# First MLP by Strassen's seven products in two tiles instead of five, with work that waits one step behind

## The chip, the cores and the metric

The kernel runs on one core of a Trainium2 chip. The metric is the device time of one execution in microseconds (us); lower is better. Before the change it is 1857.77 us, the median of three runs (1857.09 to 1859.08).

## What is computed

Linear attention over 8 batches of 8 heads (sequence 576, head size 64), whose output, 4608 tokens by 512, goes through two MLPs, all in float32:

```python
q_s = softmax over the head size of q;  k_s = softmax over the sequence of k
kv = einsum('bhsd,bhse->bhde', k_s, v);  x = einsum('bhsd,bhde->bhse', q_s, kv)   # 4608 x 512
xn = x / sqrt(mean(x * x) + 1e-6) * rms_g
g, val = xn @ w_gate, xn @ w_val                                                   # 512 x 1536 each
x = (silu(g) * val) @ w_out                                                        # 1536 x 512
h = x @ w_in; out = (h * sigmoid(1.702 * h)) @ w2_out                              # 512 x 2048, 2048 x 512
```

## The kernel before, in words

TensorE (PE) multiplies in a short float format, so each float32 factor is split into a high and a low half and each product takes three passes (high x high, high x low, low x high). VectorE (DVE), ScalarE (ACT) and GpSimd (POOL) make the halves, the sums and the nonlinear functions; SyncE (SP) issues most DMAs.

The tokens go in nine tiles of 512, numbered 0 to 8 here as in the code. A tile of the first MLP takes one of two forms.

A **plain tile** has 36 slots, three for each of the 12 blocks of 128 hidden columns: `hidden` for the gate (12 matmuls of 512 columns, L587), `hidden` for the value, then four output parts (`out1_parts`, 12 matmuls of 512 columns, also L587).

A **Strassen tile** (`strassen_tile`, L857) takes the first layer as 7 products of half blocks instead of 8. Its 6 groups `m` have 7 steps `k` each, in the order of products `p` = 1, 6, 5, 2, 7, 4, 3; a step is 12 matmuls of 256 columns (L893). After them the step's code goes to the other engines: DVE adds the product into the running sums `h` (L906), ACT takes silu of one half (L870), DVE multiplies it with the other (L871), ACT and DVE split the result `u` (L875, L879). `PARTS` says how many output parts PE does in each step. Tiles 3 to 7 are of this form (`FIRST`, `LAST`); three PSUM banks serve the products, one (`ps_att`) the attention. In plain tiles the products have two and the attention two.

Beside tile j the attention of four units (two heads of one batch each, `unit_steps`) makes the rows that the tile after needs, as nine steps s0 to s8: m of k (L364), a transpose (L371) and maxima (L375, L378), a second transpose (L383) and k less its maximum (L384), the exponentials (L402) and the quotient (L408 to L411), the product of k and v (s4, L417) and its halves (L425 to L434), transposes of q (L447) and their halves (L460, L461), and the attention product (L470 to L472), whose copy `xr` (L478) is ACT's. The tables `AT` and `AT7` place these steps in slots or steps; `EARLIER` and `ahead` move them up. `norm_steps` then squares, sums (L542), inverts (L548) and scales (L560) the tile's rows, and `split_x` (L579) or `x_sum`, `x_high` and `x_low` make the factors of the next tile.

Strassen tiles need sums of weights, made once in plain tiles by 12 `prepare_steps` (POOL L753, L760; ACT L666; DVE L667, one per prep) and stored to DRAM; before the change six of them lie in tile 1 and six in tile 2. Everything is issued in the order in which the Python code runs; each engine takes its own instructions in that order. Tile 8 and the second MLP (from L982 on) follow.

Of the kernel before, what the change touches and what calls it, by code (L numbers as in the profile page):

```python
# [20 lines left out]
def attention_glu_mlp(  # L21
# [26 lines left out]
    nc = tc.nc  # L48
# [32 lines left out]
    FIRST, LAST = 3, NTILE - 2  # L81
# [211 lines left out]

    units = [(b, c) for b in range(B) for c in range(NC)]
# [57 lines left out]
    def unit_steps(u, tag="att"):  # L352
# [16 lines left out]
        def s1():  # L369
# [5 lines left out]
            nc.vector.reduce_max(out=m, in_=t[:, 0:P], axis=AX.X)  # L375
            st["m"] = m
            qm = ap.tile([P, 2, R, 1], F32, tag="qm", bufs=2, name="qm")
            nc.vector.tensor_reduce(out=qm, in_=qt[u], op=ALU.max, axis=AX.X)  # L378
            side.tensor_tensor(qt[u], qt[u], qm.to_broadcast([P, 2, R, D]), op=ALU.subtract)

        def s2():
            t = bank(tag)
            nc.tensor.transpose(t[:, 0:P], st["m"].to_broadcast([P, P]), ident)  # L383
            nc.vector.tensor_tensor(  # L384
                kt[u],
                kt[u],
                t[:, 0:P]
                .rearrange("p (h o d) -> p h o d", h=2, o=1)
                .to_broadcast([P, 2, R, D]),
                op=ALU.subtract,  # L390
            )

        def s3():
# [12 lines left out]
            qe = st["q"]  # L406
            qs = ap.tile([P, R, 2, 1], F32, tag="qs", bufs=2, name="qs")
            nc.vector.tensor_reduce(out=qs, in_=qe, op=ALU.add, axis=AX.X)  # L408
            nc.vector.tensor_scalar_add(qs, qs, EPS_SUM)
            nc.vector.reciprocal(out=qs, in_=qs)  # L410
            side.tensor_tensor(qe, qe, qs.to_broadcast([P, R, 2, D]), op=ALU.mult)  # L411

        def s4():
            t = bank(tag)
            for r in range(R):
                for h in range(2):
# [26 lines left out]
        def qT(i):  # L443
# [17 lines left out]
            nc.vector.tensor_tensor(lo, t[:, :width], f(hi), op=ALU.subtract)  # L461
# [27 lines left out]
    def norm_steps(j):  # L489
        st = {}  # L490

        def squares(c):
# [3 lines left out]
            else:  # L496
# [32 lines left out]
        def halves_of_squares():  # L529
# [4 lines left out]
            nc.vector.tensor_tensor(st["h"][1], st["a"], f(st["h"][0]), op=ALU.subtract)  # L534

        def total():
# [7 lines left out]
            invert(0)  # L544
# [26 lines left out]
    def x_room(o):  # L571
        w = sp.tile([P, 2 * T + 16], F32R, tag="xs", bufs=4, name="xs")
# [1009 lines left out]
```

## Time and profile before

| | |
|---|---|
| median of three runs | 1857.77 us |
| the profiled execution | 1859.59 us, span 1857.8 us |
| busy: PE, PE weight loads, DVE, ACT, POOL | 93%, 84%, 68%, 47%, 31% of the span |
| the chain that ended last | PE 70%, DVE 15%, ACT 7%, DMA 3%, issue 3%, POOL 2% |
| tile 0; tiles 1 to 8; second MLP | 162.15; 980.13; 715.5 us |

The tiles' borders are the first matmul of each tile's first layer. A busy PE is not PE at its peak, since the ends of matmuls are modelled: the table of stretches gives PE 112.75 of 122.42 us in tile 2, in which PE's own work, back to back, is shorter. In the rows of stretches the engines stand in the order PE, PEld (weight loads), DVE, ACT, POOL; PEclk is the granted clock as a share of the full one. A wait is the idle time of an engine before an instruction, with what ended it.

### The profile page before, as it was taken

To read this page: it belongs to the slowest core of one execution; us is meant where nothing else is said; L and a number is where in the kernel's file an instruction comes from. 1 tells how busy PE (TensorE), PEld (TensorE's weight loads), DVE (VectorE), ACT (ScalarE), POOL (GpSimd) and SP (SyncE) were. 2 spreads that over 40 slices of the span, in tenths; PEclk is the share of its full clock that TensorE was granted. 3 is DMA by queue.
4 is the path that set the end of the run, shared out by engine and by line. 5 is a ranking of instruction groups with operands and counts; after the bars stand their busy time and mean duration, and the time that the engine had idled before them with its cause. 6 is when DMAs were issued, how large, how long until landed. Compare 5 with 4: busy or idle time off the path is not lost.

```text
span 1857.8 us, 29833 instructions
## 1 busy us (share of the span) xinstructions
PE 1733.6 (93%) x11082; PEld 1563.1 (84%) x11082; DVE 1266.1 (68%) x2079; ACT 865.3 (47%) x1491; POOL 570.1 (31%) x510
## 2 busy tenths in 40 slices
PE   6999898987988898888999999999999999999998
PEld 4666786777877787777888888999999999999998
DVE  7997878875575676675645435655555788887776
ACT  6775445445445554454333234544444643333332
POOL 5875735762252252242321162311000510000000
PEclk9999999999999999999999999999999999999999
DMA  6664534546455555554453303455434574444442
GB/s 164 189 184 127 173 110 147 174 133 184 146 171 172 163 164 174 155 174 128 119 153 114 125 30 119 162 177 180 149 128 137 190 241 130 145 135 131 131 126 80
DMA packets 292129, 275.65 MB, mean 148 GB/s; under 512 B 63504, under 2 KB 273424, under 8 KB 291984
## 3 DMA queue, kind: packets, MB, share of 16 engines
q1 hardware_dynamic: 281856, 255.92, 44.7%
q10 hardware_dynamic: 10128, 17.83, 2.6%
q8 instruction: 87, 1.43, 0.3%
q14 instruction: 58, 0.48, 0.1%
HBM read 189.27 MB, written 84.41 MB: 147 GB/s over the span
## 4 chain that ended last, share of the span: by engine, by line
PE 70%; DVE 15%; ACT 7%; DMA 3%; issue 3%; POOL 2%; SPq 0%; ACTq 0%; DVEq 0%; POOLq 0%
PE ps_out L1494 19%; PE ps_in L997 19%; PE ps_gv L587 9%; PE ps_acc L587 8%; PE ps_gv L893 7%; PE ps_third L893 5%; DVE h L906 2%; ACT L402 1%; DMA w2d<-w 1%; DVE m L364 1%; DVE s L871 1%; DVE qs L408 1%; PE ps_acc L615 1%; DVE xr L560 1%; DVE sqa L548 1%
## 5 line engine op out<-in xcount | busy, mean ns | idle before, releaser
L997 PE MATMUL ps_in<-xf,w2i 128*128 128x384 f32 x2016 | 350.3, 335 | 0.0
L997 PEld LDWEIGHTS ps_in<-xf,w2i 128*128 128x128 f32 x2016 | 349.9, 188 | 0.3 <-ACT h L1009 0.2
L587 PE MATMUL ps_acc<-u,wo 128*128 128x512 f32 x1152 | 311.7, 402 | 4.6 <-DVE u L879 4.0
L1494 PE MATMUL ps_out<-w2o,uf 128*128 128x256 f32 x2268 | 271.4, 281 | 0.0
L1494 PEld LDWEIGHTS ps_out<-w2o,uf 128*128 128x128 f32 x2268 | 269.5, 188 | 1.1
L186 POOL TENSOR_TENSOR wo<-raw,wo 128x512 fp32r<-128x512 f32 x96 | 133.1, 1387 | 408.2 <-ACT wo L185 337.7
L587 PEld LDWEIGHTS ps_acc<-u,wo 128*128 128x128 f32 x1152 | 207.7, 193 | 42.6 <-DVE u L879 6.5
L587 PE MATMUL ps_gv<-xs,wg 128*128 128x512 f32 x576 | 147.4, 403 | 5.5 <-DVE xs L579 4.8
L587 PE MATMUL ps_gv<-xs,wv 128*128 128x512 f32 x576 | 143.4, 396 | 1.4 <-POOL wv L186 1.4
L587 PEld LDWEIGHTS ps_gv<-xs,wg 128*128 128x128 f32 x576 | 108.2, 190 | 34.6 <-DVE xs L579 5.9
L587 PEld LDWEIGHTS ps_gv<-xs,wv 128*128 128x128 f32 x576 | 106.0, 188 | 26.0 <-POOL wv L186 2.9
L982 ACT ACTIVATE h<-h 128x384 f32<-128x384 f32 x144 | 74.2, 525 | 110.9 <-DVE h L1021 88.9
L870 ACT ACTIVATE s<-h 128x256 f32<-128x256 f32 x90 | 37.5, 417 | 170.5 <-DVE h L906 170.5
L182 POOL TENSOR_TENSOR w<-w,stage 128x512 int32<-128x512 int32 x56 | 76.0, 1357 | 121.0 <-DMA wv<-w1s_v 34.3
L663 DVE TENSOR_TENSOR raw<-raw 128x256 f32<-128x256 f32 (+1 forms) x236 | 106.2, 492 | 9.3 <-DMA raw<-w2d 7.3
L906 DVE TENSOR_TENSOR h<-h,ps_gv 128x512 f32<-128x512 f32 x100 | 68.1, 681 | 62.2 <-PE ps_gv L893 61.3
L1021 DVE TENSOR_TENSOR h<-h,ps_in 128x384 f32<-128x384 f32 x144 | 77.8, 553 | 48.0 <-PE ps_in L997 47.8
L1082 ACT ACTIVATE uf<-raw 128x1792 fp32r<-128x1792 f32 (+2 forms) x38 | 61.6, 1623 | 83.4 <-DVE raw L663 42.8
L1494 PE MATMUL ps_out<-w2oq,uf 128*128 128x256 f32 x756 | 90.9, 281 | 0.0
L1494 PEld LDWEIGHTS ps_out<-w2oq,uf 128*128 128x128 f32 x756 | 90.1, 188 | 0.0
L1086 DVE TENSOR_TENSOR uf<-raw,uf 128x1792 fp32r<-128x1792 f32 (+2 forms) x38 | 73.0, 1924 | 17.9 <-ACT uf L1082 17.9
L1317 ACT ACTIVATE s<-ps_gv 128x512 f32<-128x512 f32 x48 | 28.7, 599 | 115.8 <-PE ps_gv L587 115.7
(246 smaller groups left out, 3194.4 us busy)
## 6 DMA issues: line engine op xcount, KB each, us to landing
u<-h SPq DMA_DIRECT2D x192, 192.0 KB, 1.9
wg<-w1s_g SPq DMA_DIRECT2D x120, 256.0 KB, 3.9
wv<-w1s_v SPq DMA_DIRECT2D x120, 256.0 KB, 4.1
stage<-in_moe_w_out_dram SPq DMA_DIRECT2D x28, 512.0 KB, 3.7
raw<-u SPq DMA_DIRECT2D x24, 512.0 KB, 4.4
x<-ev ACTq DMA_DIRECT2D x34, 256.0 KB, 3.2
stage<-in_moe_w_in_dram SPq DMA_DIRECT2D x16, 512.0 KB, 3.8
w2d<-w SPq DMA_DIRECT2D x32, 256.0 KB, 5.0
```

Source lines behind the costliest of these rows:

```text
L182: return scaled, signed, lambda: nc.gpsimd.tensor_tensor(dst, dst, lo, op=ALU.add)
L186: nc.gpsimd.tensor_tensor(dst[:, 1, :], src, f(dst[:, 0, :]), op=ALU.subtract)
L587: nc.tensor.matmul(t, w(a), x(e), start=first and i == 0, stop=last and i == 2)
L663: engine.tensor_tensor(raw[:, o], raw[:, a], raw[:, b], op=op)
L893: nc.tensor.matmul(t[:, i * Q : (i + 1) * Q], w[:, a, c * P : (c + 1) * P], xs[j, p][0][c][:, e, :], start=p in (1, 6, 5, 4) and i == 0 an ...
L906: add = lambda o, a, t=both: nc.vector.tensor_tensor(o, a, t, op=ALU.add)
L982: nc.scalar.activation(dst, src, AF.Gelu_apprx_sigmoid)
L997: nc.tensor.matmul(t, w[:, a, s, c * P : (c + 1) * P], xfac[i, p, c][:, e, :], start=p in (1, 6, 5) and c == 0 and k == 0, stop=c == 1 and ...
L1021: nc.vector.tensor_tensor(v, v, t, op=ALU.add)
L1082: nc.scalar.activation(ufac[k][:, 0, piece], uraw[k][:, 1:8][:, piece], AF.Copy)
L1086: nc.vector.tensor_tensor(w[:, 1, piece], raw[:, piece], f(w[:, 0, piece]), op=ALU.subtract)
L1494: nc.tensor.matmul(t[:, i * Q : (i + 1) * Q], u[:, a, LEFT[p] - 1, i * P : (i + 1) * P], w[:, e, m % 2, :], start=m == 0 and i == 0 and n ...
```

## The change

Tiles 3, 4 and 5 become plain tiles; 6 and 7 stay Strassen tiles. The 12 preps lie three each in tiles 1 to 4, in slots 0 to 3, 8 to 11 and 16 to 19. In Strassen tiles `soon` puts DVE's and POOL's share of an attention step (and what follows the squares) into the next step's code, there behind that step's own add; the quotient goes two steps behind. Silu, product, high half and low half of `h` go to one later step each (`after_next`), except for product 2, whose silu and multiplication stay in its own step. `EARLIER` is 10 instead of 6 in Strassen tiles, so s4 follows product 2 (k=3) instead of product 1 (k=0); the tile before the first Strassen tile keeps 6, and plain tiles in front of plain ones have 0. The four inversions and the scaling of a Strassen tile are spread over more steps, `PARTS` starts one step later, and the rooms of the split x lose 64 bytes of padding.

```diff
-    FIRST, LAST = 3, NTILE - 2
+    FIRST, LAST = 6, NTILE - 2
...
+    late = {"now": [], "steps": False}
+
+    def soon(fn):
+
+        if late["steps"]:
+            late["now"].append(fn)
+        else:
+            fn()
+
+    def run_late():
+        now, late["now"] = late["now"], []
+        for fn in now:
+            fn()
...
-            nc.vector.reduce_max(out=m, in_=t[:, 0:P], axis=AX.X)
             st["m"] = m
-            qm = ap.tile([P, 2, R, 1], F32, tag="qm", bufs=2, name="qm")
-            nc.vector.tensor_reduce(out=qm, in_=qt[u], op=ALU.max, axis=AX.X)
-            side.tensor_tensor(qt[u], qt[u], qm.to_broadcast([P, 2, R, D]), op=ALU.subtract)
+
+            def maxima():
+                nc.vector.reduce_max(out=m, in_=t[:, 0:P], axis=AX.X)
+                qm = ap.tile([P, 2, R, 1], F32, tag="qm", bufs=2, name="qm")
+                nc.vector.tensor_reduce(out=qm, in_=qt[u], op=ALU.max, axis=AX.X)
+                side.tensor_tensor(
+                    qt[u], qt[u], qm.to_broadcast([P, 2, R, D]), op=ALU.subtract
+                )
+
+            soon(maxima)
...
-            nc.vector.tensor_tensor(
-                kt[u],
...
-                op=ALU.subtract,
+            soon(
...
+                    op=ALU.subtract,
+                )
             )
...
-            qe = st["q"]
...
-            side.tensor_tensor(qe, qe, qs.to_broadcast([P, R, 2, D]), op=ALU.mult)
+
+            def divide():
+                qe = st["q"]
+                qs = ap.tile([P, R, 2, 1], F32, tag="qs", bufs=2, name="qs")
+                nc.vector.tensor_reduce(out=qs, in_=qe, op=ALU.add, axis=AX.X)
+                nc.vector.tensor_scalar_add(qs, qs, EPS_SUM)
+                nc.vector.reciprocal(out=qs, in_=qs)
+                side.tensor_tensor(qe, qe, qs.to_broadcast([P, R, 2, D]), op=ALU.mult)
+
+            soon(lambda: soon(divide))
...
+            soon(lambda: kv_halves(t))
+
+        def kv_halves(t):
...
-            nc.vector.tensor_tensor(lo, t[:, :width], f(hi), op=ALU.subtract)
+            soon(lambda: nc.vector.tensor_tensor(lo, t[:, :width], f(hi), op=ALU.subtract))
...
-                side.tensor_tensor(st["a"], st["a"], sq, op=ALU.add)
+                soon(lambda: side.tensor_tensor(st["a"], st["a"], sq, op=ALU.add))
             if j >= 2 and c == NC - 1:
-                halves_of_squares()
+                soon(halves_of_squares)
...
-            invert(0)
+            if not late["steps"]:
+                invert(0)
...
-        w = sp.tile([P, 2 * T + 16], F32R, tag="xs", bufs=4, name="xs")
+        w = sp.tile([P, 2 * T], F32R, tag="xs", bufs=4, name="xs")
...
-            w = x_room(8).rearrange("p e (c t) -> p e c t", c=2)
+            w = x_room(0).rearrange("p e (c t) -> p e c t", c=2)
...
-    PARTS = (0, 1, 1, 2, 1, 1, 2)
...
+    PARTS = (0, 0, 1, 2, 1, 2, 2)
...
-            nc.scalar.activation(half, h[:, 0], AF.Silu)
-            return lambda: nc.vector.tensor_tensor(half, half, h[:, 1], op=ALU.mult)
+            return (
+                lambda: nc.scalar.activation(half, h[:, 0], AF.Silu),
+                lambda: nc.vector.tensor_tensor(half, half, h[:, 1], op=ALU.mult),
+            )
+
+        def after_next(*fns):
+
+
+            def one():
+                fns[0]()
+                if fns[1:]:
+                    after_next(*fns[1:])
+
+            late["now"].append(one)
...
-                later = []
+                end = []
+                now, late["now"] = late["now"], []
...
-                    later.append(hidden_part(s[1], 0, h["c1"]))
+                    after_next(*hidden_part(s[1], 0, h["c1"]))
...
-                    later.append(hidden_part(s[0], 1, both))
+                    silu, mult = hidden_part(s[0], 1, both)
+                    silu()
+                    end.append(mult)
...
-                    later.append(hidden_part(s[i], o, h[name]))
                     n, half = 2 * m + i, s[i]
-                    later.append(lambda n=n, half=half: split_high(n, half))
-                    later.append(
-                        lambda n=n, half=half: late["now"].append(lambda: split_low(n, half))
-                    )
-                run_late()
-                late["now"] += later
+                    silu, mult = hidden_part(half, o, h[name])
+
+                    def finish(mult=mult, n=n, half=half):
+                        mult()
+                        split_high(n, half)
+
+                    after_next(silu, finish, lambda n=n, half=half: split_low(n, half))
+                for fn in now:
+                    fn()
                 for _ in range(PARTS[k]):
                     if parts:
...
-                    if 7 * m + k == (4, 5, 7, 8)[c]:
+                    if 7 * m + k == (5, 6, 7, 8)[c]:
...
                 for fn in plan(7 * m + k):
+                    fn()
+                for fn in end:
                     fn()
                 aside(k)
...
-        EARLIER = 6
+        EARLIER = 10
...
-                put7(j, 35 - EARLIER, total)
-                for i in (1, 2, 3):
-                    put7(j, 35 + (i + 1) // 2 - EARLIER, invert, i)
-                put7(j, 36 - EARLIER, spread, False)
+                put7(j, 36 - EARLIER, total)
+                for i in range(4):
+                    put7(j, 37 + i - EARLIER, invert, i)
+                put7(j, 40 - EARLIER, spread, False)
                 for c in range(NC):
-                    put7(j, 37 + c // 2 - EARLIER, scale, c)
+                    put7(j, 41 + c // 2 - EARLIER, scale, c)
                 continue
-            ahead = EARLIER if by_strassen(j + 1) else 0
+            ahead = 6 if by_strassen(j + 1) else 0
...
-                put(FIRST - 1, 30 + i, x_sum, FIRST, p)
+                put(FIRST - 1, 29 + i, x_sum, FIRST, p)
...
-                x_low(FIRST, p, nc.gpsimd)
+                x_low(FIRST, p, nc.vector if p == 3 else nc.gpsimd)
...
+            put(FIRST - 1, 35, x_early, 3)
...
-                decode_aside()
+                decode_aside_soon()
...
+            late["steps"] = by_strassen(j)
...
-                        x_high(j + 1, 3)
-                        x_low(j + 1, 3, nc.gpsimd)
```

On DVE at the end of tile 1, where tile 2's input is inverted (L548, after the change L582), scaled (L560, now L594) and split (L579, now L613), there stands before:

```order
L378 TENSOR_REDUCE qm<-q_sb 128x10
L379 TENSOR_TENSOR q_sb<-q_sb,qm 128x640
L548 RECIPROCAL sqa<-sqa 128x128 x3
L384 TENSOR_TENSOR k_sb<-k_sb,ps_att 128x640
L176 TENSOR_SCALAR w_2660<-w_2660 128x512
L177 SCALAR_TENSOR_TENSOR w_2660<-stage,w_2660 128x512
L560 SCALAR_TENSOR_TENSOR xr<-xr,g_sb,sqa 128x512 x4
L408 TENSOR_REDUCE qs<-qe 128x10
L409 TENSOR_SCALAR qs<-qs 128x10
L410 RECIPROCAL qs<-qs 128x10
L411 TENSOR_TENSOR qe<-qe,qs 128x640
L579 TENSOR_TENSOR xs<-xr,xs 128x512 x4
```

and now:

```order
L582 RECIPROCAL sqa<-sqa 128x128
L1391 TENSOR_TENSOR s<-s,ps_gv 128x512
L637 CAST u<-s 128x512
L638 TENSOR_TENSOR u<-s,u 128x512
L582 RECIPROCAL sqa<-sqa 128x128 x3
L176 TENSOR_SCALAR w_2606<-w_2606 128x512
L177 SCALAR_TENSOR_TENSOR w_2606<-stage,w_2606 128x512
L594 SCALAR_TENSOR_TENSOR xr<-xr,g_sb,sqa 128x512 x4
L613 TENSOR_TENSOR xs<-xr,xs 128x512 x4
```

The next unit's maximum, its k and its quotient no longer stand between the inversion and the split; tiles 2 and 3 end in the same way now, while the end of tile 4 reads as that of tile 1 did.

On DVE in tile 6, around the halves of the product of k and v (`rs`, `kvH`, `kvL`), there stands before:

```order
L503 TENSOR_TENSOR sqa<-sqa,sqb 128x512
L879 TENSOR_TENSOR u<-s,u 128x512
L871 TENSOR_TENSOR s<-s,h 128x256
L425 TENSOR_SCALAR rs<-ps_att 128x1
L426 RECIPROCAL rs<-rs 128x1
L429 TENSOR_SCALAR kvH_78<-ps_att,rs 64x64 x2
L434 SCALAR_TENSOR_TENSOR kvL_80<-ps_att,rs,kvH_78 64x64 x2
L906 TENSOR_TENSOR h<-h,ps_gv 128x512
L879 TENSOR_TENSOR u<-s,u 128x512
L461 TENSOR_TENSOR qL<-ps_att,qH 128x320
```

and now:

```order
L899 TENSOR_TENSOR s<-s,ps_third 128x256
L946 TENSOR_TENSOR h_7332<-h,ps_gv 128x512
L946 TENSOR_TENSOR h<-h_7332,ps_gv 128x512
L454 TENSOR_SCALAR rs<-ps_att 128x1
L455 RECIPROCAL rs<-rs 128x1
L458 TENSOR_SCALAR kvH_79<-ps_att,rs 64x64 x2
L463 SCALAR_TENSOR_TENSOR kvL_81<-ps_att,rs,kvH_79 64x64 x2
L946 TENSOR_TENSOR h_7332<-h_7332,ps_third 128x512
L490 TENSOR_TENSOR qL<-ps_att,qH 128x320
```

The halves stood ahead of the add of product 6 (`h<-h,ps_gv`); they now stand behind both adds of product 7.

On ACT in tile 6, around the exponentials of k and q (L402, now L424), there stands before:

```order
L478 ACTIVATE xr<-ps_att 128x64
L478 ACTIVATE xr<-ps_att 128x256
L402 ACT_TABLE_LOAD
L402 ACTIVATE ke<-k_sb 128x2x5x64
L402 ACTIVATE qe<-q_sb 128x2x5x64
L870 ACT_TABLE_LOAD
L870 ACTIVATE s<-h 128x256
L875 ACTIVATE u<-s 128x512
L478 ACTIVATE xr<-ps_att 128x256
L501 ACTIVATE sqb<-xr 128x512
```

and now:

```order
L507 ACTIVATE xr<-ps_att 128x64
L507 ACTIVATE xr<-ps_att 128x256
L424 ACT_TABLE_LOAD
L424 ACTIVATE ke<-k_sb 128x2x5x64
L424 ACTIVATE qe<-q_sb 128x2x5x64
L507 ACTIVATE xr<-ps_att 128x256
L530 ACTIVATE sqb<-xr 128x512
L898 ACT_TABLE_LOAD
L898 ACTIVATE s<-ps_third 128x256
```

The copy `xr` of the second half of the attention rows stood behind a table load, a silu (`s<-h`) and a high half (`u<-s`); it now follows the exponentials.

On PE in tile 6, around the product of k and v (L417, now L443) and the transposes of q (L447, now L476), there stands before:

```order
L893 MATMUL ps_gv<-xs,wg_553 128x256 x6
L893 MATMUL ps_gv<-xs,wv_601 128x256 x6
L417 MATMUL ps_att<-v_sb_82,ke 64x65 x10
L893 MATMUL ps_gv<-xs,wg_663 128x256 x6
L893 MATMUL ps_gv<-xs,wv_695 128x256 x6
L587 MATMUL ps_acc<-u,wo 128x512 x3
L447 MATMUL ps_att<-ident,qe 128x128 x3
```

and now:

```order
L932 MATMUL ps_third<-xs,wg_942 128x256 x6
L932 MATMUL ps_third<-xs,wv_994 128x256 x6
L621 MATMUL ps_acc<-u,wo 128x512 x6
L443 MATMUL ps_att<-v_sb_83,ke 64x65 x10
L932 MATMUL ps_gv<-wg_1242,wg_842 128x256 x3
L932 MATMUL ps_gv<-wv_1281,wg_842 128x256 x3
L932 MATMUL ps_gv<-wg_1242,wv_881 128x256 x3
L932 MATMUL ps_gv<-wv_1281,wv_881 128x256 x3
L621 MATMUL ps_acc<-u,wo 128x512 x3
L476 MATMUL ps_att<-ident,qe 128x128 x3
```

The product of k and v stood behind product 1 and now stands behind product 2 and two output parts; the transposes stood behind product 6 and one part, now behind product 7 and one part.

## Rows read from the trace of the kernel before

**Rows 1.** Stretches, tiles 1 to 8: us, busy (count) by engine, PEclk, DMA, GB/s

```profile
162.15:282.62 120.47, 115.12 (x585) 90.15 (x584) 90.92 (x134) 60.02 (x95) 63.98 (x54) 0.99 0.44 138
282.62:405.04 122.42, 112.75 (x547) 89.64 (x546) 102.40 (x142) 59.04 (x94) 75.38 (x60) 0.99 0.48 154
405.04:539.19 134.15, 111.25 (x772) 100.00 (x770) 85.75 (x152) 65.23 (x117) 53.11 (x43) 0.94 0.55 164
539.19:672.39 133.20, 114.57 (x784) 102.44 (x782) 87.43 (x156) 67.33 (x125) 46.81 (x36) 0.94 0.56 165
672.39:805.17 132.78, 114.55 (x784) 102.48 (x782) 87.56 (x156) 67.09 (x125) 46.82 (x36) 0.94 0.55 167
805.17:934.00 128.83, 112.61 (x781) 100.68 (x780) 78.93 (x147) 61.67 (x118) 40.67 (x31) 0.95 0.47 137
934.00:1037.13 103.13, 97.08 (x652) 88.25 (x651) 49.83 (x84) 37.29 (x73) 17.87 (x14) 0.98 0.45 133
1037.13:1142.28 105.15, 105.15 (x457) 85.48 (x457) 43.19 (x74) 31.40 (x71) 38.51 (x41) 1.00 0.21 67
```

**Rows 2.** Chain that ended last: start, us, engine, tile, line, count

```profile
934.16 2.81 PE ps_gv L893 x24
...
1037.13 5.53 PE ps_gv L587 x24
```

**Rows 3.** Timeline of PE, tiles 1 and 2: start, us, what [idle before]

```profile
231.75 0.33 PE L371 MATMUL ps_third<-ident,m 128*128 128x128 f32 x1 [1.94 <-DVE qL L461]
...
231.83 4.58 PE L587 MATMUL ps_acc<-u,wo 128*128 128x512 f32 x12
...
287.31 4.25 PE L587 MATMUL ps_gv<-xs,wg 128*128 128x512 f32 x11 [4.30 <-DVE xs L579]
...
315.46 0.33 PE L371 MATMUL ps_third<-ident,m 128*128 128x128 f32 x1 [0.94 <-DVE qL L461]
...
319.57 0.32 PE L383 MATMUL ps_att<-ident,m 128*128 128x128 f32 x1 [1.01 <-DVE m L375]
```

**Rows 4.** Timeline of DVE, last slots of tile 1

```profile
222.12 2.31 DVE L667 TENSOR_TENSOR wy<-wy,wz 128x1024 fp32r<-128x1024 f32 x1
...
272.72 0.28 DVE L375 TENSOR_REDUCE m<-ps_third 128x1 f32<-128x128 f32 x1
...
274.51 2.57 DVE L548 RECIPROCAL sqa<-sqa 128x128 f32<-128x128 f32 x3
...
277.00 0.76 DVE L384 TENSOR_TENSOR k_sb<-k_sb,ps_att 128x640 f32<-128x640 f32 x1
...
284.53 0.81 DVE L408 TENSOR_REDUCE qs<-qe 128x10 f32<-128x640 f32 x1
...
286.57 2.49 DVE L579 TENSOR_TENSOR xs<-xr,xs 128x512 fp32r<-128x512 f32 x4
```

**Rows 5.** Waits of PE, 803 to 933 us (tile 6): total, times, longest

```profile
PE ps_att L417 <- ACT xr L478: 8.1, 3, 3.7
```

**Rows 6.** Waits of PE, 933 to 1037 us (tile 7)

```profile
PE ps_gv L893 <- DVE s L871: 2.9, 2, 1.8
PE ps_third L893 <- DVE s L871: 2.4, 2, 1.2
```

**Rows 7.** Timeline of DVE, second product group of tile 6

```profile
833.68 0.16 DVE L425 TENSOR_SCALAR rs<-ps_att 128x1 f32<-128x1 f32 x1 [0.24 <-PE ps_att L417]
...
834.70 0.60 DVE L434 SCALAR_TENSOR_TENSOR kvL<-ps_att,rs,kvH 64x64 fp32r<-64x64 f32 x2
...
836.61 0.69 DVE L906 TENSOR_TENSOR h<-h,ps_third 128x512 f32<-128x512 f32 x1 [1.31 <-PE ps_third L893]
...
846.48 0.81 DVE L384 TENSOR_TENSOR k_sb<-k_sb,ps_att 128x640 f32<-128x640 f32 x1
```

**Rows 8.** Line 893 by tiles: count, ns min/median/max, first and last start

```profile
L893 PE MATMUL ps_gv<-xs,wg x480: 277/281/582, 405.0 to 1024.1; 128*128 128x256 f32 x160
...
L893 PE MATMUL ps_gv<-wv,wg x180: 277/282/415, 421.2 to 1034.7; 128*128 128x256 f32 x180
```

More of the change, by code (lines that the diff above doesn't have):

```diff
@@ L383, in s2 @@
             nc.tensor.transpose(t[:, 0:P], st["m"].to_broadcast([P, P]), ident)
-            nc.vector.tensor_tensor(
-                kt[u],
[L386 to L389, printed above, removed]
-                op=ALU.subtract,
+            soon(
+                lambda: nc.vector.tensor_tensor(
+                    kt[u],
+                    kt[u],
+                    t[:, 0:P]
+                    .rearrange("p (h o d) -> p h o d", h=2, o=1)
+                    .to_broadcast([P, 2, R, D]),
+                    op=ALU.subtract,
+                )
             )
@@ L405, in s3 @@
                 load_v(u + 1)
-            qe = st["q"]
[L407 to L410, printed above, removed]
-            side.tensor_tensor(qe, qe, qs.to_broadcast([P, R, 2, D]), op=ALU.mult)
+            def divide():
[6 more added lines that the diff above has]
+            soon(lambda: soon(divide))
         def s4():
@@ L533, in halves_of_squares @@
             nc.scalar.activation(st["h"][0], st["a"], AF.Copy)
-            nc.vector.tensor_tensor(st["h"][1], st["a"], f(st["h"][0]), op=ALU.subtract)
+            soon(
+                lambda: nc.vector.tensor_tensor(
+                    st["h"][1], st["a"], f(st["h"][0]), op=ALU.subtract
+                )
+            )
         def total():
@@ L856, in x_step @@
             late["now"].append(lambda: x_low(j, p, side))
-    PARTS = (0, 1, 1, 2, 1, 1, 2)
-    late = {"now": []}
-    def run_late():
-        now, late["now"] = late["now"], []
-        for fn in now:
-            fn()
+    PARTS = (0, 0, 1, 2, 1, 2, 2)
     def strassen_tile(j, plan, parts, aside):
@@ L869, in hidden_part @@
             half = s[:, o * Q : (o + 1) * Q]
-            nc.scalar.activation(half, h[:, 0], AF.Silu)
-            return lambda: nc.vector.tensor_tensor(half, half, h[:, 1], op=ALU.mult)
+            return (
+                lambda: nc.scalar.activation(half, h[:, 0], AF.Silu),
+                lambda: nc.vector.tensor_tensor(half, half, h[:, 1], op=ALU.mult),
+            )
+        def after_next(*fns):
[4 more added lines that the diff above has]
+            late["now"].append(one)
         def split_high(n, s):
@@ L1257, in attention_glu_mlp, with decode_aside_soon, rest @@
             for i, p in enumerate((6, 7, 5, 4)):
-                put(FIRST - 1, 30 + i, x_sum, FIRST, p)
+                put(FIRST - 1, 29 + i, x_sum, FIRST, p)
             def x_early(p):
                 x_high(FIRST, p)
-                x_low(FIRST, p, nc.gpsimd)
+                x_low(FIRST, p, nc.vector if p == 3 else nc.gpsimd)
             put(FIRST - 1, 33, x_early, 7)
             put(FIRST - 1, 34, x_early, 4)
+            put(FIRST - 1, 35, x_early, 3)
+        def decode_aside_soon():
+            if at["decode"] == len(todo_pieces):
+                return
+            piece = todo_pieces[at["decode"]]
+            scaled, signed, finish = decode_parts()
+            scaled()
+            def rest():
+                signed()
+                finish()
+                decoded.append((piece, halves.pop(piece)))
+                fetch_next()
+            soon(rest)
         def aside(k):
             if k == 1:
-                decode_aside()
+                decode_aside_soon()
             elif k == 4:
```

## Prediction

> **What bounds the kernel now.** I cut the span into its nine tiles and the second MLP and read one row for each tile [rows 1], then ask in each what PE does when nothing holds it. For that the chain of waits gives two stretches without a gap [rows 2]: 24 matmuls of 512 columns in 5.53 us, 0.2304 each, and 24 of 256 columns in 2.81 us, 0.1171 each. A plain tile's first layer is 288 of the former, 66.4 us; a Strassen tile's is 504 of the latter, 59.0 us; the output parts are 144 x 0.2304 = 33.2 us in both. So the seven products save 7.3 us of PE's work per tile, and a tile needs 99.6 or 92.2 us beside attention.
>
> The reader is to set these against the durations [rows 1]. Tile 8, plain and without attention, carries 24 matmuls more (the last parts of tile 7): 105.1 by the price, 105.15 measured, so PE alone bounds it. Tile 7, Strassen without attention, is 103.13 against 92.2: 11 us lost. Tiles 1 and 2, plain with attention and six preps each, are 120.47 and 122.42 against 99.6: 21 and 23 us for attention's matmuls and waits. Tiles 3 to 6, Strassen with attention, are 134.15, 133.20, 132.78 and 128.83 against 92.2: 37 to 42 us. The granted clock says the same: 0.98 to 0.99 in tiles 1 and 2, 0.94 to 0.95 in 3 to 6. **With attention beside it, the Strassen form is the slower one**: it saves 7.3 us of matmuls and loses 15 us and more to waits. Two reasons show. It has one PSUM bank for attention where plain tiles have two, and PE waits there for ACT's copy of the attention rows, 8.1 us in three waits in tile 6 [rows 5]; and its products wait for the multiplication of silu, 2.9 and 2.4 us in tile 7 [rows 6]. After a longer wait comes slow clock: behind a wait of 1.94 us twelve matmuls take 4.58 us instead of 2.77 [rows 3], 1.8 us on top.
>
> **The change part by part.**
>
> Tiles 3, 4, 5 become plain. I take tile 2 as the model, 122.42 us [rows 1], and correct it.
> (a) Its first matmuls wait 4.30 us for the split x, and eleven then take 4.25 us instead of 2.53 [rows 3]: 6.0 us. In DVE's queue between the inversion and the split stand the next unit's maxima (272.72 to 274.51, 1.8 us), its k (0.76) and its quotient (284.53 to 286.57, 2.0) [rows 4], 4.6 us together, and the split starts where the wait ends. With `ahead` 0 they stand behind, so the ends of tiles 1, 2 and 3 lose this wait but for some 0.5 us; the end of tile 4 keeps it.
> (b) Its second and third units wait before both transposes, 0.94 + 1.01 us for the first such pair [rows 3] and as much again for the other. A prep's subtraction of 1024 columns, 2.31 us long while POOL adds [rows 4], stands in DVE's queue ahead of them. With preps in slots 0 to 3 and 8 to 11 both pairs stay; the pair after slot 15, 1.94 us and 1.8 us of slow clock in tile 1 [rows 3], goes, and I leave 0.5 us.
> So tiles 2, 3 and 4: 122.4 - 6.0 + 0.5 - 0.9 (a wait before the sums for Strassen, which only the last plain tile makes) + 0.5 = 116.5, taken as 117 each. Tile 1: 120.5 - 3.7 - 1 (a unit's first steps leave it) = 116. Tile 5 has no preps (4 us less) but all the sums for tile 6, the work of one and a half units of tile 6 at its end (2 us of PE, and I give it 2 us of waits), and tile 4's late split ahead of it: 122. Together 116 + 3 x 117 + 122 = 589 against 643.0 (the first five of rows 1): **-54 us**. Bounds: each plain tile as slow as tiles 1 and 2 now, 5 x 121.5 = 607 (-35); all pairs gone, 5 x 114 = 570 (-73).
>
> Tile 6. Removed: the waits for `xr`, 8.1 us [rows 5], since ACT's copy no longer stands behind a silu that waits for DVE; the slow clock after them, up to 0.05 x 128.83 = 6.4 us by the granted 0.95 [rows 1]; the waits for the multiplication, about 4 us at tile 7's price [rows 6], since that of product 2 no longer stands behind product 7's adds. About 19 us. Added: deferred reads hold the one attention bank. The halves of k times v take 833.68 to 835.30, 1.6 us [rows 7], and stand now behind both adds of product 7 (0.69 each [rows 7]), so 3.0 us after that product; PE has one output part (0.69) to do before it needs the bank: 2.3 us of wait. The subtraction from k (0.81 [rows 7]) stands behind product 6's add, a multiplication of 256 columns (0.4, estimated from the add of 512) and a low half of 512 (as the add): 0.69 + 0.4 + 0.69 + 0.81 = 2.6 us after a product that no part follows. Three units, 3 x 4.9 = 14.7 us; with 3 to 5 us of slow clock it is 18 to 20, and without it 15; what moved into tile 5 is 2 us. Below, the waits could all fall under other work: -19; above, slow clock after each of six: +8. I take **-5 us** (124), near the balance, since the moved work and part of the slow clock are the rest. The queue order is what this hangs on. [...] The trace agrees as far as it goes: the split in (a) starts right behind the quotient ahead of it [rows 4].
>
> Tile 7 has no units. The multiplication of product 2 now has product 7 and parts to hide behind: of 11 us lost, 5.3 [rows 6] and one slow stretch go. **-6 us** (97), between -1 and -9.
>
> Without price: the rooms of x 4096 bytes apart. Matmuls that stream from the padded rooms take 281 ns, those that stream from the weights' rooms, which are 4096 bytes long, 282 [rows 8]; between -0.5 and +0.5 us per tile. The fetches of weight sums of three tiles go from SP's queue; no row has PE waiting for them, so nothing is counted. Tile 8 and the second MLP have the same code. Tiles 0 and 8 and the second MLP stay at 162.15, 105.15 and 715.5 us.
>
> Sum: -54 - 5 - 6 = -65. The profiled execution took 1859.59 us, 1.8 more than its span and than the median of 1857.77; taken from the median, 1793 us.
>
> **The rivals.**
> *The deferral costs nothing in tile 6.* DVE is idle when the reads come and the parts cover them; tile 6 is then about 110, and the time is 1857.8 - 54 - 19 - 6 = 1779. For it: DVE is busy only 78.93 of 128.83 us there [rows 1]. Against it: the waits are of order, not of load.
> *The plain tiles stay as slow as tiles 1 and 2 now.* Three preps per tile still put a long subtraction before a pair of transposes, and POOL's adds stretch DVE's work: 607 for tiles 1 to 5; with tile 6 at 124 or a little worse and tile 7 at 97, 1857.8 - 35 - 5 - 6 = 1812. For it: 102.40 us of DVE in 122.42 [rows 1].
> *The loss is attention's and not Strassen's: slower.* If what tiles 3 to 5 lose came from their units, data or DMAs, plain tiles there would keep the waits and add 7.3 us each of PE's work: +22, and with tiles 6 and 7 unchanged 1880 us. It decides once a plain tile in that place takes over 133.4 us, the mean of the three. Against it: tiles 1 and 2 run the same units at 120.47 and 122.42. [...]
> *The change does not do what it says.* If the deferred work came into the same place, tile 6 would stay at 128.83 and the time at 1798; this lies within the forecast's own width.
>
> **How the numbers follow.** Forecast 1793 with its own width (1785 to 1803): 0.50. Deferral free, 1779: 0.20. Plain tiles as slow as now, 1812: 0.25. Slower, 1880: 0.03; something else, near no change: 0.02. The range reaches to both faster cases and their spread, 1768 to 1816, and leaves out the slower one and the far tails. Three runs of this kernel spread by 0.1%, so about 0.2% can be told from no change. Faster by more than that: 0.95, same 0.02, slower 0.03.
>
> **What would show it.** Right: the first five tiles' stretches sum to near 589 us with the granted clock at 0.98 or more; at the ends of tiles 1 to 3 no wait for the split x over 1 us, at the end of tile 4 one of about 4 us; in tile 6 no wait of L443 for `xr`, but waits of about 2.3 us before L476 for `kvL` and of about 2.6 us before L499 for k; in tile 7 no wait for the multiplication. Wrong: plain tiles at 120 us or over, tile 6 under 115 or over 131, or waits of L476 and L499 that are absent.

## The result

The changed kernel takes 1800.51 us, the median of four runs (1798.27 to 1800.92); the kernel before takes 1858.42 us beside it. The ratio is 0.9685, 95% interval 0.9668 to 0.9702. The profiled execution has a span of 1798.3 us against 1857.8, so 59.5 us went.

The stretches of the changed kernel, tiles 1 to 8, answer to [rows 1]; columns: from:to and length in us, then busy us (count) of PE, PEld, DVE, ACT, POOL, the granted clock as a share, DMA share, GB/s:

```profile
161.70:275.34 113.64, 111.67 (x565) 88.98 (x563) 78.72 (x128) 54.91 (x90) 44.55 (x36) 1.00 0.38 114
275.34:389.62 114.28, 110.71 (x568) 89.53 (x566) 84.48 (x136) 55.30 (x87) 44.79 (x37) 1.00 0.37 117
389.62:503.79 114.17, 110.99 (x567) 89.38 (x566) 84.57 (x136) 55.29 (x87) 44.90 (x37) 1.00 0.38 117
503.79:619.55 115.76, 112.03 (x589) 90.17 (x588) 87.04 (x140) 57.46 (x93) 43.48 (x36) 1.00 0.37 113
619.55:742.28 122.73, 113.94 (x573) 92.20 (x572) 85.94 (x148) 56.30 (x96) 36.43 (x28) 0.97 0.33 96
742.28:877.59 135.31, 110.81 (x745) 99.69 (x744) 84.01 (x132) 56.48 (x109) 43.70 (x32) 0.92 0.43 125
877.59:979.76 102.17, 95.86 (x651) 87.59 (x650) 53.81 (x85) 36.68 (x70) 17.81 (x14) 1.00 0.45 134
979.76:1083.38 103.62, 103.62 (x457) 85.52 (x456) 43.18 (x75) 31.92 (x72) 38.44 (x41) 1.00 0.21 67
```

| us | before | predicted | after |
|---|---|---|---|
| tiles 1 to 5 | 643.0 | 589 | 580.6 |
| tile 6 | 128.8 | 124 | 135.3 |
| tile 7 | 103.1 | 97 | 102.2 |
| tile 8 | 105.2 | 105.2 | 103.6 |

The rows of before count tile 1 from 162.15 and tile 8 from 1037.13; their first matmuls lie at 161.58 and 1036.97. Counted as in the changed kernel, tiles 1 to 5 gave 0.6 us more than the table says and tile 7 0.2 less.

The plain tiles gave 62.4 us. **Tile 6 did not get shorter but 6.5 us longer**, at a granted clock of 0.92 where it had 0.95, and tile 7 gave 1 us. What PE waits for in tile 6 (total us, times, longest):

```profile
PE ps_att L499 <- DVE k_sb L405: 7.8, 3, 3.5
PE ps_att L476 <- DVE kvL L463: 7.3, 3, 2.4
PE ps_acc L621 <- DVE u L918: 4.2, 3, 2.2
PE ps_att L403 <- DVE qL L490: 2.6, 1, 2.6
PE ps_att L476 <- DVE m L392: 1.3, 1, 1.3
PE ps_att L385 <- DVE qL L490: 1.3, 1, 1.3
```

The waits for `xr` [rows 5] and for the multiplication are gone. In their place stand the two that the prediction had named, and below them three that it had not. In tile 7:

```profile
PE ps_acc L621 <- DVE u L918: 5.9, 4, 2.4
PE ps_gv L932 <- DVE s L899: 0.2, 1, 0.2
```

The 5.3 us of [rows 6] fell to 0.2, and 5.9 us of another wait came: output parts wait for the low half of `u`. Before, that low half stood ahead of product 6's add in DVE's queue (L879 ahead of L906):

```profile
968.46 0.69 DVE L879 TENSOR_TENSOR u<-s,u 128x512 fp32r<-128x512 f32 x1
...
969.87 0.69 DVE L906 TENSOR_TENSOR h<-h,ps_gv 128x512 f32<-128x512 f32 x1 [0.40 <-PE ps_gv L893]
```

Now it (L918) stands behind that add (L946) and a multiplication (L899), and PE, after product 5, comes to the part before it is done (timelines of DVE, POOL and PE):

```profile
913.11 0.69 DVE L946 TENSOR_TENSOR h<-h,ps_gv 128x512 f32<-128x512 f32 x1 [2.97 <-ACT u L914]
913.71 1.48 DVE L899 TENSOR_TENSOR s<-s,h 128x256 f32<-128x256 f32 x1
915.11 1.46 DVE L918 TENSOR_TENSOR u<-s,u 128x512 fp32r<-128x512 f32 x2
913.62 1.29 POOL L186 TENSOR_TENSOR wo<-raw,wo 128x512 fp32r<-128x512 f32 x1 [7.47 <-ACT wo L185]
915.85 0.74 PE L621 MATMUL ps_acc<-u,wo 128*128 128x512 f32 x2 [1.18 <-DVE u L918]
```

In three of the four waits, each of 1.18 us, the multiplication takes 1.48 us while an instruction of POOL runs (L186 here); in the other three groups it takes 0.41 or 0.42 us. In the fourth wait, of 2.38 us, a split of x (L613) stands ahead of the add as well.

In tile 3, one of the new plain tiles:

```profile
PE ps_gv L621 <- DVE xs L613: 1.2, 1, 1.2
PE ps_third L385 <- DVE qL L490: 0.9, 1, 0.9
PE ps_att L385 <- DVE qL L490: 0.8, 1, 0.8
```

How one of the new waits in tile 6 comes about, on DVE and then on PE (timelines: start, us, what, [idle before]):

```profile
759.66 0.69 DVE L946 TENSOR_TENSOR h<-h,ps_gv 128x512 f32<-128x512 f32 x1 [0.41 <-PE ps_gv L932]
760.38 0.69 DVE L946 TENSOR_TENSOR h<-h,ps_third 128x512 f32<-128x512 f32 x1
760.99 0.15 DVE L454 TENSOR_SCALAR rs<-ps_att 128x1 f32<-128x1 f32 x1
...
762.01 0.60 DVE L463 SCALAR_TENSOR_TENSOR kvL<-ps_att,rs,kvH 64x64 fp32r<-64x64 f32 x2
```

```profile
757.20 0.80 PE L443 MATMUL ps_att<-v_sb,ke 128*64 128x65 f32 x20
...
759.46 0.86 PE L621 MATMUL ps_acc<-u,wo 128*128 128x512 f32 x3
762.75 0.53 PE L476 MATMUL ps_att<-ident,qe 128*128 128x128 f32 x3 [2.43 <-DVE kvL L463]
```

The product of k and v is done at 758. Its reader on DVE (L454) starts at 760.99, behind both adds of the product after it (L946), for the first of which DVE waits 0.41 us on PE. PE has one output part to do, needs the bank at 760.3 and gets it at 762.75.

### The profile page after: what moved, and what is told of

Read it like the earlier page. It is cut to its first block, busy times and chain, and to the rows that moved or that the text cites. A ratio compares the mean times of both kernels' runs of the same rounds, so it can differ in the third digit from the quotient of the medians.

```text
span 1798.3 us, 27948 instructions
## 1 busy us (share of the span) xinstructions
PE 1721.0 (96%) x10434; PEld 1528.3 (85%) x10434; DVE 1240.7 (69%) x2009; ACT 820.5 (46%) x1383; POOL 501.9 (28%) x454
## 4 chain that ended last, share of the span: by engine, by line
PE 55%; DVE 2%; DMA 0%; ACT 0%; issue 0%; DVEq 0%
PE ps_out L1555 20%; PE ps_in L1043 19%; PE ps_acc L621 6%; PE ps_gv L932 4%; PE ps_gv L621 4%; PE ps_third L932 2%; DVE h L946 1%; DVE s L899 1%; DVE u L918 0%; DMA x<-ev 0%; DVE y L1569 0%; PE ps_att L476 0%; PE ps_att L443 0%; DVE kvL L463 0%; DVE kvH L458 0%
## 5 line engine op out<-in xcount | busy, mean ns | idle before, releaser
L621 PE MATMUL ps_acc<-u,wo 128*128 128x512 f32 x1152 | 298.5, 401 | 11.3 <-DVE u L918 10.1
L621 PEld LDWEIGHTS ps_acc<-u,wo 128*128 128x128 f32 x1152 | 211.7, 192 | 58.2 <-DVE u L918 13.2
L621 PE MATMUL ps_gv<-xs,wg 128*128 128x512 f32 x1008 | 252.5, 398 | 8.1 <-DVE xs L613 7.4
L186 POOL TENSOR_TENSOR wo<-raw,wo 128x512 fp32r<-128x512 f32 x96 | 134.3, 1399 | 417.8 <-ACT wo L185 365.3
L621 PE MATMUL ps_gv<-xs,wv 128*128 128x512 f32 x1008 | 248.4, 394 | 1.1 <-POOL wv L186 1.0
L621 PEld LDWEIGHTS ps_gv<-xs,wg 128*128 128x128 f32 x1008 | 188.3, 190 | 55.2 <-DVE xs L613 9.7
L621 PEld LDWEIGHTS ps_gv<-xs,wv 128*128 128x128 f32 x1008 | 185.6, 188 | 40.7 <-POOL wv L186 2.7
L1380 ACT ACTIVATE s<-ps_gv 128x512 f32<-128x512 f32 x84 | 50.3, 599 | 238.5 <-PE ps_gv L621 238.3
L1391 DVE TENSOR_TENSOR s<-s,ps_gv 128x512 f32<-128x512 f32 x84 | 56.9, 677 | 95.2 <-PE ps_gv L621 86.8
L432 DVE TENSOR_REDUCE qs<-qe 128x10 f32<-128x640 f32 x32 | 26.2, 819 | 73.0 <-ACT qe L424 72.9
```

The costliest lines, as they stand in the source:

```text
L186: nc.gpsimd.tensor_tensor(dst[:, 1, :], src, f(dst[:, 0, :]), op=ALU.subtract)
L621: nc.tensor.matmul(t, w(a), x(e), start=first and i == 0, stop=last and i == 2)
L1391: nc.vector.tensor_tensor(s, s, tv, op=ALU.mult)
```

## The experiments

Unless said otherwise a run changes the changed kernel. Tiles are in us, each from one profiled execution. Tile 5 is the same code in the change, soon_off, kv_k_now, parts_later and now_and_later, and takes 121.2 to 125.6 us there, at a granted clock of 0.95 to 0.99 in the first four; so in a tile below full clock a difference of under 4 us is not put down to an edit. Tile 2, at full clock and with the same code, takes 114.28 us in the change and in preps_only.

| run | time, us | ratio to before, 95% interval | tile 5 | tile 6 | tile 7 |
|---|---|---|---|---|---|
| the change | 1800.51 | 0.9685 (0.9668 to 0.9702) | 122.7 | 135.3 | 102.2 |
| count_only | 1791.62 | 0.9636 (0.9620 to 0.9653) | 113.6 | 133.5 | 101.4 |
| order_only | 1908.50 | 1.0270 (1.0254 to 1.0285) | 145.4 | 135.9 | 101.9 |
| soon_off | 1788.55 | 0.9620 (0.9606 to 0.9635) | 121.2 | 122.7 | 103.4 |
| kv_k_now | 1787.58 | 0.9618 (0.9602 to 0.9634) | 123.9 | 121.7 | 102.0 |
| parts_later | 1788.24 | 0.9617 (0.9603 to 0.9631) | 125.6 | 126.9 | 96.1 |
| now_and_later | 1777.19 | 0.9558 (0.9544 to 0.9572) | 122.2 | 117.8 | 96.2 |
| one_tile | 1757.43 | 0.9454 (0.9439 to 0.9470) | 114.2 | 115.1 | 92.9 |
| no_strassen | 1739.08 | 0.9352 (0.9338 to 0.9366) | 109.9 | 109.8 | 98.4 |
| preps_only | 1755.09 | 0.9437 (0.9423 to 0.9451) | 110.0 | 109.7 | 98.4 |
| preps_six | 1757.17 | 0.9450 (0.9436 to 0.9464) | 109.9 | 109.8 | 98.4 |
| padded | 1745.53 | 0.9387 (0.9373 to 0.9401) | 110.3 | 110.4 | 100.1 |

### Which half of the change gave the time

**count_only**, an edit of the kernel before:

```diff
-    FIRST, LAST = 3, NTILE - 2
+    FIRST, LAST = 6, NTILE - 2
```

> The kernel before with two Strassen tiles (6 and 7) and nothing else of the change. Theory A (the whole gain is the three tiles that became plain, and the work put one step behind makes tile 6 slower): tiles 1 to 5 sum to 580 to 587 us as after the change, tile 6 returns to about 129 us from 135.3, tile 7 about 103: 1790 to 1799 us in all, faster than the changed kernel. Theory B (tile 6 is slow because it is now the first Strassen tile behind plain ones, and the order of the work costs nothing): tile 6 stays at 134 us or more, 1800 to 1808 us.

It is 8.9 us faster than the whole change: the fewer Strassen tiles gave 67 us, and the rest of the change (the new order, and the rooms without padding) took 9 of them back. But tile 6 was not at 129; in that Theory B was right. Tile 5 is 113.6 us here (tiles 1 to 5 sum to 572.8, below theory A's 580 to 587) and 122.7 after the change, which gave it the first units of tile 6: PE waits there for `m` of k (`PE ps_third L385 <- DVE m L378: 5.4, 2, 3.6`). Tile 6, with less to do, got no shorter for it. Its stretch in count_only, and two of its waits in the old line numbers (L417 is the product of k and v, L447 the transposes of q):

```profile
734.68:868.17 133.49, 111.37 (x769) 100.01 (x768) 78.30 (x143) 60.15 (x114) 47.20 (x38) 0.92 0.45 134
```

```profile
PE ps_att L417 <- ACT xr L478: 9.9, 3, 4.6
PE ps_att L447 <- POOL qe L411: 4.6, 1, 4.6
```

Behind a plain tile the old order gives a tile 6 of 133.5 us: the `xr` waits are 9.9 us, not 8.1, and the first unit's quotient on POOL is late once by 4.6 us. The 128.83 of [rows 1] was the tile behind another Strassen tile, and was no base for the tile that the change leaves.

**order_only**:

```diff
-    FIRST, LAST = 6, NTILE - 2
+    FIRST, LAST = 3, NTILE - 2
```

> The changed kernel with five Strassen tiles (3 to 7) again: all of the change but the count. Theory A: tiles 3 to 6 each get 5 to 10 us slower than in the kernel before (134, 133, 133, 129), with waits of about 2.4 us for the halves of k times v and 2.6 us for k in each unit: 1875 to 1895 us. Theory B: tiles 3 to 6 are as long as before or shorter: 1840 to 1858 us.

With five Strassen tiles the new order is 50 us slower than the old, and 13 us beyond theory A's range: tiles 3 to 5 lose 10 to 13 us each, not 5 to 10, and tile 2, with the early units beside six preps, comes to 133.4 us. Tiles 3 to 5 are 144 to 146 us each where they had 133 to 134; tile 4's stretch and its longest waits:

```profile
558.22:704.57 146.35, 119.62 (x784) 106.40 (x783) 90.35 (x157) 66.56 (x124) 48.82 (x36) 0.90 0.50 151
```

```profile
PE ps_att L476 <- DVE kvL L463: 10.0, 4, 2.7
PE ps_att L499 <- DVE k_sb L405: 8.8, 3, 3.5
```

So the order as it stands is a loss where attention runs beside Strassen's products, and the gain of the change is the plain tiles.

### Which late piece it is

**soon_off**:

```diff
-        if late["steps"]:
-            late["now"].append(fn)
-        else:
-            fn()
+        fn()
```

> The changed kernel in which the attention's, the squares' and the decoding's work on DVE and POOL stays in its own step (the function soon calls at once); silu and the split of u keep their later steps. Theory A: the waits for the halves of k times v and for k (15.1 us in tile 6) go or fall under 4 us, slow clock falls from 20.5 us of half clock to under 14; tile 6 comes to 118 to 128 us, 1783 to 1793 us in all. Theory C (reading at once only moves the wait to ACT's and DVE's products, as in the kernel before): tile 6 at 128 us or more, 1793 to 1800 us.

Tile 6 falls by 12.6 us and the time by 12.0. The two named waits are not all gone: 5.1 us of 15.1 stay, where theory A gave under 4, and the granted clock rises only from 0.92 to 0.94.

**kv_k_now**, in which only the two reads of the bank that the prediction priced stand in their own step:

```diff
-            soon(lambda: kv_halves(t))
+            kv_halves(t)
...
-            soon(
-                lambda: nc.vector.tensor_tensor(
-                    kt[u],
...
+            nc.vector.tensor_tensor(
+                kt[u],
```

> The changed kernel in which only two of the late pieces stand in their own step again: the halves of k times v and the subtraction from k. Theory A1 (it is these two reads of the one attention bank that make tile 6 long): their waits, 15.1 us in tile 6, fall under 5 us, half clock falls from 20.5 us to 14 or less, tile 6 to 121 to 126 us, and the time to 1786 to 1792 us, as with everything at once (1788.6). Theory E (it is the others, the maxima, the halves of q and the quotient, or slow clock by itself): 1796 to 1801 us.

Theory A1 holds: these two pieces alone give back 12.9 us, as much as all of them together; the lateness of the quotient and the squares costs nothing that can be measured, and neither do the halves of q and the maxima on balance. What PE still waits for in tile 6 (line numbers two lower here):

```profile
PE ps_acc L619 <- DVE u L916: 4.8, 4, 2.2
PE ps_att L403 <- DVE qL L488: 2.6, 1, 2.6
PE ps_att L385 <- DVE qL L488: 2.5, 2, 1.9
...
PE ps_att L474 <- DVE kvL L461: 1.3, 1, 1.3
```

The wait for `kvL` is 1.3 us in place of 7.3, and the one for k is gone. The low halves of `u` are left.

**parts_later**:

```diff
-    PARTS = (0, 0, 1, 2, 1, 2, 2)
+    PARTS = (0, 0, 0, 2, 2, 2, 2)
```

> The changed kernel with the output parts of a group one step later again (none behind the first three products, two behind each of the other four). Theory F (the parts behind the third product come before the low half of u, since that now follows two steps behind the multiplication): the wait of the parts for u, 5.9 us in tile 7 and 4.2 in tile 6, goes; tile 7 falls from 102.2 to 93 to 97 us and tile 6 changes by less than 5: 1788 to 1796 us. Theory G (another wait takes its place at once): tile 7 at 100 us or more, 1797 to 1802 us.

Theory F holds for tile 7, 102.2 to 96.1 us. Its waits:

```profile
PE ps_acc L621 <- DVE u L918: 0.9, 1, 0.9
PE ps_gv L932 <- DVE s L899: 0.5, 1, 0.5
```

Tile 6 falls by 8.4 us, more than the 4.2 of that wait and than the 5 that theory F allowed; its granted clock rises from 0.92 to 0.96, while that of tile 5, whose code is unchanged, falls from 0.97 to 0.95. How much of the 8.4 us belongs to the edit is open.

**now_and_later**, the edits of soon_off and parts_later together:

> The changed kernel with both repairs: attention's work at once and the output parts one step later. If the two remove different waits (12.0 and 12.3 us, theory L): 1773 to 1780 us, tile 6 at 114 to 119 us and tile 7 at 96. If the two remove the same waits or the same slow clock (theory M): 1783 to 1789 us.

Theory L: 23.3 us against 12.0 + 12.3. The two repairs remove different waits. Tiles 6 and 7, both at full clock:

```profile
742.71:860.53 117.82, 102.61 (x746) 92.28 (x745) 85.49 (x132) 56.66 (x109) 42.82 (x32) 1.00 0.48 144
860.53:956.70 96.17, 94.70 (x652) 87.61 (x650) 53.31 (x85) 36.00 (x70) 16.93 (x14) 1.00 0.47 142
```

### Whether the Strassen form pays at all

**no_strassen** (the second edit leaves out the restoring of weights that no prep has overwritten):

```diff
-    FIRST, LAST = 6, NTILE - 2
+    FIRST, LAST = 8, NTILE - 2
...
-            if j == LAST + 1:
+            if j == LAST + 1 and FIRST <= LAST:
```

> The changed kernel with no Strassen tile: tiles 6 and 7 plain, no preps, no sums of weights. If the form costs more than it saves wherever it stands (theory A): tiles 1 to 5 at 113 to 114.5 us each, tile 6 at 112 to 115, tile 7 at about 100, tile 8 at about 100 since no parts are left over: 41 us less than the changed kernel, 1755 to 1768 us. If the seven products do pay in the two tiles (theory D: 7.3 us of matmuls saved in each, the rest being attention's waits that a plain tile has too): 1800 to 1815 us.

The fastest version: 61 us less than the change, 20 more than theory A's 41. Tiles 2, 6 and 7:

```profile
272.08:381.84 109.76, 109.62 (x568) 89.80 (x566) 76.06 (x133) 52.19 (x85) 24.05 (x18) 1.00 0.29 85
711.50:821.28 109.78, 109.64 (x568) 89.81 (x567) 73.00 (x128) 48.16 (x81) 18.27 (x14) 1.00 0.16 48
821.28:919.69 98.41, 98.41 (x436) 81.46 (x434) 33.76 (x53) 23.87 (x40) 15.56 (x12) 1.00 0.03 11
```

PE is busy for the whole of each tile. Tile 6 is 25.5 us shorter than by Strassen, tile 2 4.5 us shorter without its preps, tile 5 12.8 us shorter without the sums for tile 6 and the early unit.

**preps_only** puts the 12 preps back into no_strassen, three in each of tiles 1 to 4:

```diff
-        if FIRST <= LAST:
             preps = [prepare_steps(kind, m) for m in range(NPAIR) for kind in "gv"]
-            each = -(-len(preps) // (FIRST - 1))
+            each = 3
```

> All tiles plain, as in the kernel with no Strassen tile (1739.1 us), but with the 12 preps, three in each of tiles 1 to 4, whose sums nobody reads. Theory H (what tiles 1 to 4 lose against 109.8 to 110.6 us is the preps): they come to 113.5 to 116 us each, and the time to 1752 to 1759 us. Theory I (the preps lie beside PE's work, and the tiles' 4 us come from something else): 1738 to 1742 us.

Theory H: 16.0 us for twelve preps; tiles 1 to 4 are 113.6, 114.3, 114.1 and 114.4 us, the first three as in the changed kernel, the fourth 1.4 us shorter, since tile 5's first unit no longer starts in it.

**preps_six**, the same with `each = 6`:

> All tiles plain with the 12 preps, six in each of tiles 1 and 2 as in the kernel before, whose sums nobody reads. If a prep has the same price as with three in a tile (theory N: 16 us for twelve): tiles 1 and 2 at 117 to 119 us, 1753 to 1757 us. If six crowd each other on POOL and DVE (theory O, the prediction's second rival carried on): tiles 1 and 2 at 121 us or more, 1760 to 1768 us.

Between the two theories: tiles 1 and 2 come to 119.8 and 120.1 us, at a granted clock of 0.99, and all twelve cost 18.1 us. Six in a tile crowd each other a little, by 2 to 3 us in all.

**one_tile** has FIRST at 7 and the parts of parts_later:

> One Strassen tile only, tile 7, which has no attention beside it, with two preps in each of tiles 1 to 6, and the output parts one step later. Theory A (even at its best place the form does not earn its preps): tile 7 at 94 to 97 us against 98.4 plain, but 15 to 17 us for the 12 preps and 3 to 10 for the sums of x at the end of tile 6: 1753 to 1766 us. Theory J (two preps in a tile lie beside PE's work and cost nothing): 1735 to 1745 us.

Theory A again. Tiles 6 and 7:

```profile
727.00:842.12 115.12, 110.55 (x545) 89.91 (x544) 79.43 (x126) 50.02 (x87) 43.29 (x35) 0.99 0.27 84
842.12:935.05 92.93, 91.93 (x639) 85.36 (x638) 54.91 (x84) 33.80 (x66) 18.30 (x15) 1.00 0.48 143
```

Tile 7 does 132 output matmuls here where the plain tile does 144 and leaves the other twelve to tile 8. With them (12 x 0.227) it would be 95.7 us, 2.7 less than plain; 96.2 in now_and_later, which does 144, says the same. That is what is left of the prediction's 7.3. Part of the rest is the price itself: the first layer's matmuls start 0.120 us apart at 256 columns (36 in 4.31 us at the start of tile 7 of the changed kernel) and 0.227 us at 512 (no_strassen), so 504 of the ones save 4.9 us against 288 of the others. Against it tile 6, which makes the sums, is 5.3 us longer, and tiles 1 to 5 are 2 to 4 us longer each. Where the form does pay, its own preparation costs more.

### The rooms of x

**padded**, an edit of no_strassen:

```diff
-        w = sp.tile([P, 2 * T], F32R, tag="xs", bufs=4, name="xs")
+        w = sp.tile([P, 2 * T + 16], F32R, tag="xs", bufs=4, name="xs")
```

> All tiles plain, with the 64 bytes of padding back in each room of the split x. The prediction gave the rooms no price, between -0.5 and +0.5 us per tile: with eight tiles that PE alone bounds, 1735 to 1743 us and 109.3 to 110.3 us for a tile with attention. Rival (the distance of the rooms decides how fast matmuls stream): more than 2% on the 2592 matmuls of 512 columns that read them, 12 us or more either way.

6.5 us slower: outside what the prediction allowed, and half of what the rival asked for. PE in tile 7, without a wait, padded first and then not:

```profile
842.14 2.92 PE L621 MATMUL ps_gv<-xs,wg 128*128 128x512 f32 x12
844.89 2.94 PE L621 MATMUL ps_gv<-xs,wv 128*128 128x512 f32 x12
847.67 2.71 PE L621 MATMUL ps_acc<-u,wo 128*128 128x512 f32 x11
```

```profile
834.88 2.88 PE L621 MATMUL ps_acc<-u,wo 128*128 128x512 f32 x12
837.60 2.88 PE L621 MATMUL ps_gv<-xs,wg 128*128 128x512 f32 x12
840.32 2.88 PE L621 MATMUL ps_gv<-xs,wv 128*128 128x512 f32 x12
```

From start to start twelve take 2.75 and 2.78 us with padding and 2.72 and 2.72 without, 230 against 227 ns each.

## Why the prediction held, and where it did not

**The time was foretold within 8 us, but by errors that cancelled, which is luck**: the plain tiles gave 8.4 us more than their term, and tiles 6 and 7 gave 16.5 less; tile 8 and the rest, held unchanged, gave 2.6. That makes 59.5 us in place of 65. The other 2.2 us are that the changed kernel's median lies so much above the span of its profiled execution, and the forecast was taken from a median that lay on the span.

**Tiles 1 to 5 (-54, measured -62.4).** The mechanism stands: tiles 3, 4 and 5 as plain tiles are 114.2, 115.8 and 122.7 us, at full clock but for tile 5's 0.97. Of step (a) the waits for the split x are 1.2 us at the ends of tiles 1 to 3, where I left 0.5 and named 1 as the most, and 3.3 us at the end of tile 4, where I said about 4. The mis-sized term is (b): of the pairs only the first transposes still wait, about 1 us for each of two pairs [rows 3], and the second transposes do not. That leaves 1.7 to 2.2 us a tile, where I had 3.9 and 0.5 more for the pair after slot 15. The 4 us that I took off tile 5 for having no preps were right: three cost 4.0 us, twelve 16.0 in preps_only. So was tile 5 at 122.

**Tile 6 (-5, measured +6.5).** At 135.3 us it is over the 131 that the prediction itself named as wrong. The added waits were right to half a microsecond: 6.9 us for the halves of k times v, measured 7.3 (at most 2.43 each, 2.3 foretold); 7.8 us for k, measured 7.8 (three waits, 3.5 the longest, 2.6 foretold for each). kv_k_now shows that they are the loss, since undoing these two gives 12.9 us. They come from the order of DVE's queue. That a ready read of the bank does not pass an add that waits for PE I took as given, and no run shows it as a rule. What the trace shows is the case above: the product is done at 758, DVE waits 0.41 us on PE for the first add, and the read (L454) starts at 760.99, behind both adds. What failed is the rest of the sum. The removed waits did go, 12 us. But I counted the slow clock as removed (6.4 us by 0.95) and put 3 to 5 back; at 0.92 it is up to 0.08 x 135.3 = 10.8 us, about 7 more. And three waits had no term: for the low halves of `u` 4.2, for the halves of q 3.9 and for the maxima 1.3, together 9.4, where before the waits of this kind in tile 6 were 2.6 (`kvL` 1.2, `u` 0.9, `m` of k 0.5). These two, up to 14 us, cover the miss of 11.5; how it divides between them is an estimate. The base was wrong besides: a tile 6 behind a plain tile takes 133.5 us in the old order, in which tile 5 takes 113.6; tiles 5 and 6 together are 247.1 in count_only and 258.0 after the change.

**Tile 7 (-6, measured -1).** The multiplication no longer makes PE wait, as foretold, and the clock is full. The step that failed is that I looked at the waits that go and not at those that `after_next` makes. It moves the low half that the first part reads by one step, from product 1's to product 6's, and `PARTS` moves the first part by one step too, from product 6's to product 5's; the count of steps between them is as before. But product 1 has no add on DVE and product 6 has one: the low half now stands behind that add and a multiplication, and PE has only product 5's twelve matmuls before the part. (The expectation of parts_later, that the low half follows two steps behind the multiplication, is wrong: it is one step, as before.) parts_later shows what a step more is worth: 6.0 us in tile 7 from seven numbers.

**The rooms (0, measured about 0.6 us in a plain tile with attention, 1.7 without).** Tile 8 is 1.5 us shorter [rows 1] with the same code, at 227 instead of 230 ns a matmul; I had read the times of single matmuls [rows 8], not the distance from start to start, which is what a tile is made of.

**The rivals.** "The deferral costs nothing" fell with tile 6 at 135.3. "The plain tiles stay as slow" fell with 114 us; preps_six shows that six preps would have kept them near 120. "Attention's loss and not Strassen's" fell most clearly: without Strassen the tiles with attention are bounded by PE alone (in tile 2 of no_strassen it is busy 109.62 of 109.76 us). By columns of matmuls done, 202,752 in the Strassen tile's 133.20 us (504 x 256 + 144 x 512) against 221,184 in tile 2's 122.42 (432 x 512), the plain tile was already the better used one. "The change does not do what it says", at 1798, gives a time closer to the measured one than the forecast does, and is wrong: the late work did move, as the timeline shows, and the kernel without it (count_only) is 9 us faster. The total alone could not have told these apart.

**What I did not ask**: the price showed 7.3 us to gain per Strassen tile and 15 or more lost, and I followed the change to two such tiles without pricing none.

## What to carry to other kernels

When work is put one step behind so that no engine waits for it, list everyone who needs its result or its buffer: with a single bank, the read that frees the bank must not stand in the queue behind work that waits for PE (here two such reads, 12.9 us in kv_k_now). Moving a producer and its consumer by the same number of steps is not enough: look at what stands ahead of the producer in its new place, and leave the consumer that much time (here one line of seven numbers, 12 us). And before tuning the schedule of a form that saves matmuls, run the plain form once: here the 7 us of matmuls to be saved in a tile were eaten by preparation, hand-over and waits, and the plain form is 61 us faster.

## What was not expected of the hardware

Sixty-four bytes of padding in the rooms of x change PE's pace in plain tiles: 227 ns from start to start without it, 230 with it, and 6.5 us in the whole kernel. The output parts, which read `u` and not these rooms, show it too: in tile 7 ten of their matmuls start 231 ns apart in padded (839.83 to 842.14 us) and twelve 227 ns apart in no_strassen (834.88 to 837.60 us). Whether that is the address of the rooms themselves or of what is allocated behind them was not separated.

The granted clock did not follow the sum of PE's waits: in tile 6 it was 0.92 with 24.5 us of waits listed after the change, 0.94 in kv_k_now with 13.9, and 1.00 in now_and_later, where the list still has 15.1 us, none longer than 2.6. Tile 5 says the same: PE waits there 5.4 us in all for `m` and 3.3 us for the split x both in the change and in soon_off, and its granted clock is 0.97 and 0.99. What decides between these the runs do not show, so a price for slow clock is best taken with both ends.
